# Seven block products for the output matmuls of the last pass of a retention and two-layer MLP kernel

## The chip, the core and the metric

One core of a Trainium2 chip runs the kernel. The engines are TensorE (PE in the profile, with its weight loads as PEld), VectorE (DVE), ScalarE (ACT), GpSimd (POOL) and SyncE (SP), whose queue issues nearly all the DMAs. The metric is the device time of one run in microseconds, the median of several runs; lower is better.

## What is computed

A retention layer, then two MLP layers over 2304 tokens of width 512; all in float32.

```python
x = attn_out.transpose(0, 2, 1, 3).reshape(2304, 512)     # retention, 4 x 8 heads of 576 x 64
g = x @ w_gate; x = (g * sigmoid(g) * (x @ w_val)) @ w_out   # layer one, hidden width 1536
h = maximum(x @ w_in, 0); out = (h * h) @ w_out              # layer two, hidden width 2048
```

The change lies in layer two, in the product `(h * h) @ w_out` of one third of the tokens.

## The kernel before

Every float32 operand of a matmul is held as two halves in the matmul's own 32-bit format, `hi` (a cast by ACT) and `lo` (source minus `hi`, a subtraction by DVE); `split` makes both. A product of two such operands is three matmuls: hi by hi, hi by lo, lo by hi (`three`). Inputs and results of both layers live transposed in one SBUF tile `xy`.

Layer two works in three passes of 768 tokens, each over eight systems, k = 0 to 7, of 256 hidden columns. A system's 512-deep product with `w_in` is done by Strassen's scheme in Winograd's form: seven block products P1 to P7 (`slot`), each of six matmuls of 384 columns, in the PSUM tiles `g`, `z` and `v`. The seven weight operands `wi` of a system were built in the first pass and stored in DRAM (`win`); the later passes load them one system ahead into two buffers each. After each block product ACT or DVE moves the sum out of PSUM into `cag` and `cbg` (one for the first 384 tokens, one for the others); the last two, P4 and P3, are followed by relu and square. `hidden` then splits the two halves of the tokens into `ho_hi` and `ho_lo`.

The output product is plain: `out2` takes the hidden columns of two systems (512 of them, four rows of 128) and 128 tokens, and makes twelve matmuls of 512 columns in one bank `oacc`, with weights `wo` (split once, stored as `wsp`); one instruction then adds the bank to `xy` (for the first pair, ACT copies it). A pair of systems has six such tiles, `which` "a" or "b" by j = 0 to 2. They are emitted among the block products of the following systems, by the table `outs`; the last pair's come after the last system.

The order on each engine is fixed when the program is built: the code's order, rearranged by a scheduler that goes by its own estimate of times. On the chip every engine takes its instructions in that order and waits at each one until its operands are ready.

In the names below, S0 to S7 are the eight systems of the last pass. The numbers behind names in the order listings only tell tiles apart.

Of the kernel before, what the change touches and what calls it, by code (L numbers as in the profile page):

```python
# [9 lines left out]
F32 = mybir.dt.float32  # L10
F32R = mybir.dt.float32r
U16 = mybir.dt.uint16
U32 = mybir.dt.uint32
# [48 lines left out]
def retention_moe_kernel(  # L62
# [16 lines left out]
        )  # L79

    keep = pool(ctx, "keep", 1)
    raw_p = pool(ctx, "raw_p", 2)
    cv_p = pool(ctx, "cv_p", 3)
    mid = ExitStack()
    ctx.enter_context(mid)
    cv2_p = pool(mid, "cv2_p", HOLD - 2)
    wb_p = pool(mid, "wb_p", 2)
    raw2_p = pool(mid, "raw2_p", 1)
# [286 lines left out]

    later = []
    wi_p = pool(ctx, "wi_p", 2, side="right")
    s1_p = pool(ctx, "s1_p", 1, side="right")
    xs_p = pool(ctx, "xs_p", 4, side="right")
    xo_p = pool(ctx, "xo_p", 1, side="right")  # L380

    with ExitStack() as st:
        const = pool(st, "const", 1)
# [226 lines left out]
    chain["on"] = False  # L610


    c4_p = pool(ctx, "c4_p", 1, side="right")
    ps_g2 = pool(ctx, "ps_g2", 1, space=PSUM)
    ps_a = pool(ctx, "ps_a", 1, space=PSUM)
    late = True
# [32 lines left out]
    def slot(n, i):  # L649
# [2 lines left out]
        m = M[ph]  # L652
        s = sys_.setdefault(n, {})

        if i == 1:
# [106 lines left out]
    def out2(n, which, j):  # L762

        ph, p, k, what = systems[n]
        t0 = TOKENS[ph, p]["ab".index(which)] + j * P
        final = n == len(systems) - 1 and which == "b" and j == 2
        for at in (slice(0, 256), slice(256, 512)) if final else (slice(0, 512),):
            o = out_bank()[:, at]
            for r in range(4):
                w = wos[2 * k - 2 + r]  # L770
                h = [x[:, r % 2, j * P:(j + 1) * P] for x in hid[n - 1 + r // 2, which]]
                three(o, h, (w[:, 0, at], w[:, 1, at]), r == 0, r == 3)
            home = xy[:, at.start // P:at.stop // P, t0:t0 + P]
            src = o.rearrange("p (c q) -> p c q", q=P)
            if k == 1:
                act.copy(home, src)
            else:
                tt(out=home, in0=src, in1=home, op=ALU.add)
            if k == F2 // 2 - 1:
                sp.dma_start(out=out[t0:t0 + P, at].rearrange("p (c q) -> p c q", q=P), in_=home)  # L780

    flip = systems.index((2, 0, 0, "i"))
    outs, fetch = {}, {}
    for n, (ph, p, k, what) in enumerate(systems):
        if what == "v":
            for x, which in enumerate("acb" if p == 0 else "ab"):
                at = n + 3 if which == "b" and n < flip - 1 else n + 2
                outs.setdefault(at, []).extend((out1, n, which, cc) for cc in range(CC))
            for f in range(2):
                fetch.setdefault((n, 1 + f), []).append((n, (2 * k + f,)))  # L790
        if what == "i":
            fetch.setdefault((n + 1 + (k + p == 0), 0), []).append((n, range(2 * k, 2 * k + 2)))
        if what == "i" and k % 2:
            for x, which in enumerate("ab"):
                outs.setdefault(n + 2 + x, []).extend((out2, n, which, j) for j in range(3))

    def after(n, i):

# [13 lines left out]
    place[:] = [dve.last, dve.last]  # L812
    pumped["limit"] = 10 ** 6
    end = len(systems)
    for n in range(end + 4):
        ph, p, k, what = systems[n] if n < end else (0, None, 0, "")
        tiles = outs.get(n, [])
        cuts = [len(tiles) * x // 3 for x in range(4)] if n != flip + 1 else [0] + 3 * [len(tiles)]
# [20 lines left out]
            spare.clear()  # L839
        for x in fetch.get((n, 0), []):  # L840
            load_out(*x)
        for x in seq:
            if x in (0, 1, 2):
                for y in fetch.get((n, x), []) if x else ():
# [5 lines left out]
            if n == flip + 1 and i == 4:  # L850
                while min(raw_t, default=len(order)) < loads["shut"] or min(w_t, default=len(order)) < loads["shut"]:
                    next(convert)
                mid.close()
                ho_p = pool(ctx, "ho2_p", 3)
                wo_p = pool(ctx, "wo2_p", 8)
            if not 0 <= k < end:
                continue
            if isinstance(i, tuple):
# [2 lines left out]
                slot(k, i)  # L861
            next(make, None)
            place[:] = place[1:] + [dve.recent]
            if (ph, p) in PACE:
                first, early, later_ = PACE[ph, p]
                pace["due"] += early if n - systems.index((ph, p, 0, ("gv", "i")[ph - 1][0])) < first else later_
                pump(int(pace["due"]))
                pace["due"] %= 1
            after(k, i)
        for _ in make:  # L870
            pass
        if (ph, p) == (2, 0) and systems[n + 1][1]:
            for _ in convert:
                pass


# [59 lines left out]
```

## Time and profile before

| | us |
|---|---|
| median of three runs | 874.51 |
| the three runs | 874.38, 874.51, 875.0 |
| span of the profiled execution | 875.1 |
| PE busy in it | 863.9 |
| DVE, ACT, POOL busy in it | 642.8, 400.9, 122.2 |
| longest wait of PE in it | 2.2 |

The span of the profiled execution is 0.6 us over the median of the runs; the slowest of them is about as long as it. In the rows, times are microseconds unless marked ns, and a matmul's duration contains its way through the array: the next one starts long before it has ended, so pitches are read from start to start.

### The profile page before, as it was taken

To read this page: it belongs to the slowest core of one execution; us is meant where nothing else is said; L and a number is where in the kernel's file an instruction comes from. 1 tells how busy PE (TensorE), PEld (TensorE's weight loads), DVE (VectorE), ACT (ScalarE), POOL (GpSimd) and SP (SyncE) were. 2 spreads that over 40 slices of the span, in tenths; PEclk is the share of its full clock that TensorE was granted. 3 is DMA by queue.
4 is the path that set the end of the run, shared out by engine and by line. 5 is a ranking of instruction groups with operands and counts; after the bars stand their busy time and mean duration, and the time that the engine had idled before them with its cause. 6 is when DMAs were issued, how large, how long until landed. Compare 5 with 4: busy or idle time off the path is not lost.

```text
span 875.1 us, 13516 instructions
## 1 busy us (share of the span) xinstructions
PE 863.9 (99%) x5064; PEld 746.0 (85%) x5064; DVE 642.8 (73%) x1002; ACT 400.9 (46%) x709; POOL 122.2 (14%) x135
## 2 busy tenths in 40 slices
PE   9989999999999999999999999999999999999998
PEld 7878888888888888888888899989899988998987
DVE  3899999998976899677647999999534467533544
ACT  3657777565544544644325466554233233232310
POOL 3343343223130010000002311120000000000000
PEclk9999999999999999999999999999999999999999
DMA  9994777755554489878745388988666465656412
GB/s 337 402 356 160 253 249 249 264 186 211 196 192 154 139 282 379 297 273 288 253 141 185 144 315 328 361 304 313 206 239 215 126 226 210 190 202 204 164 41 73
DMA packets 75218, 203.62 MB, mean 233 GB/s; under 512 B 7696, under 2 KB 18448, under 8 KB 75152
## 3 DMA queue, kind: packets, MB, share of 16 engines
q1 hardware_dynamic: 74720, 202.34, 65.8%
q8 instruction: 40, 0.66, 0.3%
q10 hardware_dynamic: 432, 0.41, 0.1%
q14 instruction: 26, 0.21, 0.1%
HBM read 138.23 MB, written 64.49 MB: 232 GB/s over the span
## 4 chain that ended last, share of the span: by engine, by line
PE 86%; DVE 7%; DMA 4%; issue 2%; ACT 1%; SPq 0%; POOL 0%; DVEq 0%; POOLq 0%; ACTq 0%
PE oacc L113 42%; PE g L113 24%; PE v L113 12%; PE z L113 6%; DVE w L113 3%; DMA qk_sb<-in_qk 3%; DVE wi L113 1%; PE o L113 1%; DMA k_sb<-in_kv 1%; DMA qs_sb<-in_qscale 1%; PE s L113 1%; DVE xy L113 1%; DVE cbg L113 0%; PE kv L113 0%; DVE xo_l L113 0%
## 5 line engine op out<-in xcount | busy, mean ns | idle before, releaser
L113 PE MATMUL g<-xo_h,wi 128*128 128x384 f32 (+1 forms) x768 | 238.3, 364 | 0.0
L113 PE MATMUL oacc<-wo,ho_hi 128*128 128x512 f32 (+1 forms) x584 | 179.5, 388 | 0.0
L113 PEld LDWEIGHTS g<-xo_h,wi 128*128 128x128 f32 x768 | 142.5, 188 | 17.1
L113 PE MATMUL oacc<-ho_hi,wo 128*128 128x512 f32 (+1 forms) x480 | 151.1, 370 | 0.5 <-ACT xy L113 0.5
L113 DVE TENSOR_TENSOR xy<-oacc,xy 128x512 f32<-128x512 f32 (+1 forms) x155 | 99.6, 648 | 59.6 <-PE oacc L113 59.1
L113 PE MATMUL g<-xo_l,wi 128*128 128x384 f32 (+1 forms) x384 | 139.6, 364 | 0.0
L113 PEld LDWEIGHTS oacc<-wo,ho_hi 128*128 128x128 f32 x584 | 108.4, 188 | 19.2
L113 PE MATMUL v<-xo_h,wi 128*128 128x512 f32 (+1 forms) x384 | 123.2, 364 | 0.0
L113 PE MATMUL oacc<-wo,ho_lo 128*128 128x512 f32 (+1 forms) x292 | 113.3, 390 | 0.0
L113 PEld LDWEIGHTS oacc<-ho_hi,wo 128*128 128x128 f32 x480 | 88.1, 188 | 17.6 <-ACT xy L113 1.3
L113 PE MATMUL oacc<-ho_lo,wo 128*128 128x512 f32 (+1 forms) x240 | 89.1, 371 | 0.0
L113 PEld LDWEIGHTS g<-xo_l,wi 128*128 128x128 f32 x384 | 72.1, 188 | 8.4
L113 DVE TENSOR_SCALAR w<-w 128x512 f32<-128x512 f32 (+1 forms) x136 | 64.9, 480 | 18.0 <-ACT w L113 17.0
L113 PEld LDWEIGHTS v<-xo_h,wi 128*128 128x128 f32 x384 | 71.2, 188 | 8.0
L113 DVE TENSOR_TENSOR cbg<-v,cbg 128x384 f32<-128x384 f32 (+1 forms) x72 | 43.1, 598 | 45.8 <-ACT cbg L113 24.3
L113 ACT ACTIVATE cag<-g 128x384 f32<-128x384 f32 (+1 forms) x36 | 19.0, 528 | 125.2 <-PE g L113 125.1
L113 PE MATMUL v<-xo_l,wi 128*128 128x512 f32 (+1 forms) x192 | 69.8, 363 | 0.0
L113 PEld LDWEIGHTS oacc<-wo,ho_lo 128*128 128x128 f32 x292 | 54.8, 188 | 11.2
L113 PE MATMUL z<-xo_h,wi 128*128 128x512 f32 (+1 forms) x192 | 62.5, 365 | 0.0
L113 ACT CAST ho_hi<-cbg 128x768 fp32r<-128x768 f32 (+1 forms) x36 | 32.7, 908 | 45.5 <-DVE cbg L113 44.4
L113 DVE SCALAR_TENSOR_TENSOR w<-raw,w 128x512 uint32<-128x512 uint32 x68 | 52.5, 773 | 0.7
L113 PEld LDWEIGHTS oacc<-ho_lo,wo 128*128 128x128 f32 x240 | 45.1, 188 | 8.7
(90 smaller groups left out, 1295.6 us busy)
## 6 DMA issues: line engine op xcount, KB each, us to landing
wi<-win SPq DMA_DIRECT2D x84, 512.0 KB, 4.2
raw<-in_w SPq DMA_DIRECT2D x68, 512.0 KB, 4.9
win<-wi SPq DMA_DIRECT2D x60, 512.0 KB, 3.6
wo<-wsp SPq DMA_DIRECT2D x44, 512.0 KB, 6.4
wsp<-wo SPq DMA_DIRECT2D x28, 512.0 KB, 5.2
qk_sb<-in_qk SPq DMA_DIRECT2D x15, 576.0 KB, 7.4
wst<-w SPq DMA_DIRECT2D x32, 256.0 KB, 6.0
wi<-win SPq DMA_DIRECT2D x28, 256.0 KB, 5.4
```

Source lines behind the costliest of these rows:

```text
L113: i = op(*args, **kw)
```

## The change

In the last pass, the output product of the first three pairs of systems (`PAIRED = 6`) is done with Winograd's seven block products too; the fourth pair stays plain. Hidden columns and output columns are cut in two, and so are the tokens: block j pairs 128 tokens of the first half with the 128 of the second. For each block there are seven products of six matmuls with 256 columns (`out3`), 126 matmuls in place of a pair's 72. The stationary sides are seven sums of the hidden blocks: POOL makes four of them, in four additions in a row for each block j (`sums2`, into a part of `xy` that is free by then), and `prepare` splits the seven in three pieces of 512, 256 and 1024 columns into `hs_h` and `hs_l`, of which there are two sets. The moving sides `wt` are weights and sums of weights: three slices of `wsp`, and four sums that POOL makes during the second pass (`operand_sums`), which are split and stored to DRAM there (`tsp`). Each product leaves a running sum in one half of a PSUM bank, which DVE adds to `xy` (ACT copies some of the first pair's) before the next product may go on in it.

The hidden tiles of the last pass, `caa` and `cab`, get pools of their own, opened when the second pass's tiles are given up; so the last system of the second pass is now finished before S0's tiles are written. Once the output tiles of the second pass are through, the 21 moving operands of the first three systems are loaded in a row (256 KB each). The block products of S0 to S3 stand ahead of the output products: `flow` lets the first of them go 25 slots into the pass, then three for every two slots. The fourth pair has `out4`, as `out2` before, with `whole` for its splits.

```diff
+PRODUCTS = (1, 5, 6, 3, 7, 2, 4)
+SUMS = (6, 5, 4, 7)
+PAIRED = 6
+START = 4
...
+        if i == 1 and n >= turn_over:
+            s["x"] = bank("g")[:, :m]
+            s["a"], s["b"] = block_tiles(n)
...
     def hidden(n, which, c):
+        if n >= turn_over:
+            return
...
+    def operand2(n, i):
+        w = moving[n, i] = t_p.tile([P, 2, 256], F32R, tag=f"t{i}", name="wt")
...
+    def operand_sums(n):
+        sums(n)
+        yield
+        yield
+        for x in range(4):
+            w = cv_p.tile([P, 512], U32, tag="w", name="tw").bitcast(F32R).rearrange("p (y q) -> p y q", y=2)
+            split(w[:, 0], w[:, 1], raw_o[n][x // 2][:, x % 2 * 256:][:, :256])
+            yield
+            soon(2, lambda x=x, w=w: sp.dma_start(out=tsp[systems[n][2]][:, x], in_=w.bitcast(F32)))
+            if x == 3 and systems[n][2] + 1 < PAIRED:
+                fetch_raw(n + 1)
+
+    def sums2(n, j):
+        a, b = (x[:, :, :, j * P:(j + 1) * P] for x in pairs_of[n])
+        a11, a12, a21, a22 = (x[:, :, f] for x in (a, b) for f in range(2))
+        sums_of[n, j] = s = xy[:, :, 2 * P * j:2 * P * (j + 1)].rearrange("p i (s q) -> p i s q", q=P)
+        for x, y, z, op in ((0, a21, a22, ALU.add), (2, a11, a21, ALU.subtract),
+                            (1, s[:, 0], a11, ALU.subtract), (3, a12, s[:, 1], ALU.subtract)):
+            pool_e.tensor_tensor(out=s[:, x], in0=y, in1=z, op=op)
+
+    def prepare(n, j):
+        a, b = (x[:, :, :, j * P:(j + 1) * P] for x in pairs_of[n])
+        hi, lo = (hl_p.tile([P, 7, 2, P], F32R, tag=x, name=f"hs_{x}") for x in "hl")
+        halves[n, j] = hi, lo
+        split(hi[:, 0:2], lo[:, 0:2], a.rearrange("p s f q -> p f s q"))
+        split(hi[:, 2], lo[:, 2], b[:, :, 1])
+        split(hi[:, 3:7], lo[:, 3:7], sums_of[n, j])
+
+    def out3(n, j, at):
+        i = PRODUCTS[at]
+        if at < 2:
+            bank_ = (2, 1 + j % 2 * 2)[at == 0]
+            banks[at] = ps_a.tile([P, 512], F32, tag=f"a{bank_}", name="oacc")
+        o = banks[at % 2 if at < 6 else 0]
+        o = o[:, 256:] if i == 2 else o[:, :256]
+        x = (1, 2, 4, 5, 6, 7, 3).index(i)
+        for s in range(2):
+            hi, lo = (z[:, x, s] for z in halves[n, j])
+            th, tl = (moving[n - 1 + s, i][:, y] for y in range(2))
+            for y, (c, d) in enumerate(((hi, th), (hi, tl), (lo, th))):
+                pe.matmul(
+                    o, c, d, start=i in (1, 5, 2) and s + y == 0, stop=s == 1 and y == 2, skip_group_check=True
+                )
...
+        if k == 1 and i in (1, 5, 6, 4):
+            act.copy(home, src)
+        else:
+            tt(out=home, in0=src, in1=home, op=ALU.add)
...
+    def ready_halves():
+        while queue and prepared["n"] < flowed["out"] + 2:
+            n, j = queue.pop(0)
+            (whole if n == end - 1 else prepare)(n, j)
+            prepared["n"] += 1
...
+    begin_at = 7 * 3 + START
+    for n in range(turn_over, end + 1):
+        seq = [(1, n), (7, n - 1), (2, n), (4, n - 1), (6, n), (3, n - 1), (5, n)]
+        if n == turn_over:
+            seq = [(7, n - 1), (4, n - 1), (3, n - 1), None, (1, n), (2, n), (5, n), (6, n)]
...
+            if i == 3 and k >= turn_over and systems[k][2] % 2:
+                for j in range(3):
+                    if k < turn_over + PAIRED:
+                        sums2(k, j)
+                    queue.append((k, j))
+                ready_halves()
...
+            flow(min(int(1.5 * (slots["n"] - begin_at)), 21 * PAIRED // 2))
+            after(k, i)
+            if n == turn_over + 1 and not tiles and t_p is None:
+                second.close()
+                front.close()
+                t_p, hl_p = pool(ctx, "t_p", 3), pool(ctx, "hl_p", 2)
+                block_pools.append(pool(ctx, "cb_p", 1, side="right"))
+                for m in range(turn_over, turn_over + 3):
+                    for i_ in PRODUCTS:
+                        operand2(m, i_)
```

On PE, behind S1's last block product P3 (`v_7484`, whose last matmul is the first row), the order before has an output tile of the pair before, then S2's P5.

```order
L113 MATMUL v_7484<-xo_h_7344,wi_7342 128x384
L113 MATMUL oacc_7591<-wo_7099,ho_hi_7213 128x512 x2
L113 MATMUL oacc_7591<-wo_7099,ho_lo_7214 128x512
L113 MATMUL oacc_7591<-wo_7101,ho_hi_7213 128x512 x2
L113 MATMUL oacc_7591<-wo_7101,ho_lo_7214 128x512
L113 MATMUL oacc_7591<-wo_7236,ho_hi_7338 128x512 x2
L113 MATMUL oacc_7591<-wo_7236,ho_lo_7339 128x512
L113 MATMUL oacc_7591<-wo_7238,ho_hi_7338 128x512 x2
L113 MATMUL oacc_7591<-wo_7238,ho_lo_7339 128x512
L113 MATMUL v_7606<-xo_h_7227,wi_7417 128x384
```

In the changed kernel S1's P3 (`v_7725`) is followed by S3's P1 (`g_7825`, six matmuls), by the first output products P1 of blocks 0 and 1 (`oacc_7871` and `oacc_7978`, twelve matmuls, of which the last ones are the first rows here), by S2's P6 (`g_7732`, six), and then by the output product P5 of block 0 (`oacc_7889`).

```order
L122 MATMUL oacc_7978<-wt_7656,hs_l_7809 128x256
L122 MATMUL oacc_7978<-wt_7670,hs_h_7808 128x256 x2
L122 MATMUL oacc_7978<-wt_7670,hs_l_7809 128x256
L122 MATMUL g_7732<-xo_h_7382,wi_7723 128x384
L122 MATMUL g_7732<-xo_l_7383,wi_7723 128x384
L122 MATMUL g_7732<-xo_h_7382,wi_7723 128x384 x2
L122 MATMUL g_7732<-xo_l_7383,wi_7723 128x384
L122 MATMUL g_7732<-xo_h_7382,wi_7723 128x384
L122 MATMUL oacc_7889<-wt_7658,hs_h_7800 128x256 x2
L122 MATMUL oacc_7871<-wt_7660,hs_h_7800 128x256 x2
L122 MATMUL v_7904<-xo_h_7377,wi_7761 128x384
```

No output tile of an earlier pair is left at this place, and between P3's last matmul and the first one that needs POOL's sums (`oacc_7889`) stand 24 others.

On POOL the order before ends with the weight sums of the first pass of layer two.

```order
L113 TENSOR_TENSOR w_in_5611<-w_in_5611 128x256
L113 TENSOR_TENSOR s1_5978<-w_in_5779 128x256
L113 TENSOR_TENSOR w_in_5779<-w_in_5778,w_in_5779 128x256
L113 TENSOR_TENSOR w_in_5778<-s1_5978,w_in_5778 128x256
L113 TENSOR_TENSOR w_in_5778<-w_in_5778 128x256
```

In the changed kernel the weight sums `w_o` of the second pass follow, and then the hidden sums of the three pairs; the first pair's twelve are these, after the last `w_o`. Of block 0 they are the first, second, seventh and tenth.

```order
L122 TENSOR_TENSOR w_o_7105<-w_o_7105,w_o_7104 128x256
L122 TENSOR_TENSOR xy_78<-cab_7489 128x256
L122 TENSOR_TENSOR xy_78<-caa_7488,cab_7489 128x256
L122 TENSOR_TENSOR xy_78<-cab_7489 128x256
L122 TENSOR_TENSOR xy_78<-caa_7488,cab_7489 128x256
L122 TENSOR_TENSOR xy_78<-cab_7489 128x256
L122 TENSOR_TENSOR xy_78<-caa_7488,cab_7489 128x256
L122 TENSOR_TENSOR xy_78<-xy_78,caa_7488 128x256 x3
L122 TENSOR_TENSOR xy_78<-caa_7488,xy_78 128x256 x3
```

The scheduler has put the three blocks side by side, so that the fourth sum of block 0 has nine others in front of it.

On DVE, in the output work behind the last system, the order before has one addition for every twelve matmuls and nothing else.

```order
L113 TENSOR_TENSOR ho_lo_8261<-cbg_8095,ho_hi_8260 128x768
L113 TENSOR_TENSOR xy_78<-oacc_8278,xy_78 128x4x128
L113 TENSOR_TENSOR xy_78<-oacc_8293,xy_78 128x4x128
L113 TENSOR_TENSOR xy_78<-oacc_8308,xy_78 128x4x128
L113 TENSOR_TENSOR xy_78<-oacc_8323,xy_78 128x4x128
```

In the changed kernel there is an addition for every six matmuls, and among them stand the three subtractions of the third pair's last block (`hs_l_8634`).

```order
L122 TENSOR_TENSOR xy_78<-oacc_8541,xy_78 128x2x128
L122 TENSOR_TENSOR hs_l_8634<-caa_7919,hs_h_8633 128x512
L122 TENSOR_TENSOR xy_78<-oacc_8657,xy_78 128x2x128
L122 TENSOR_TENSOR hs_l_8634<-cab_7920,hs_h_8633 128x256
L122 TENSOR_TENSOR xy_78<-oacc_8649,xy_78 128x2x128
L122 TENSOR_TENSOR hs_l_8634<-xy_78,hs_h_8633 128x1024
L122 TENSOR_TENSOR xy_78<-oacc_8706,xy_78 128x2x128
L122 TENSOR_TENSOR xy_78<-oacc_8657,xy_78 128x2x128
```

The additions that free a PSUM half now share DVE with the splits of the next block.

## Rows read from the trace of the kernel before

**Rows 1.** The page: span, busy time of each engine, granted clock by slices.

```profile
span 875.1 us, 13516 instructions
PE 863.9 (99%) x5064; PEld 746.0 (85%) x5064; DVE 642.8 (73%) x1002; ACT 400.9 (46%) x709; POOL 122.2 (14%) x135
PEclk9999999999999999999999999999999999999999
```

**Rows 2.** PE's waits, the longest: total, times, longest.

```profile
PE s L113 <- DMA qk_sb<-in_qk: 2.6, 2, 2.2
...
PE oacc L113 <- ACT xy L113: 0.9, 3, 0.4
```

**Rows 3.** Stretches: busy time by engine (instructions), granted clock, DMA share, GB/s.

```profile
720.00:740.00 20.00, 20.00 (x102) 18.10 (x101) 16.29 (x23) 8.37 (x14) 0.00 (x0) 1.00 0.61 226
...
760.00:780.00 20.00, 20.00 (x101) 17.99 (x100) 6.64 (x10) 6.25 (x12) 0.00 (x0) 1.00 0.69 232
780.00:800.00 20.00, 20.00 (x103) 18.30 (x103) 8.89 (x13) 7.69 (x13) 0.00 (x0) 1.00 0.61 198
```

**Rows 4.** Chain of work in the last pass: start, us, engine, matmuls.

```profile
740.71 5.49 PE oacc L113 x24
...
748.28 2.08 PE v L113 x12
...
756.31 2.77 PE oacc L113 x12
```

**Rows 5.** Timeline of PE in the last output tile: start, us, instruction.

```profile
868.15 0.62 PE L113 MATMUL oacc<-wo,ho_hi 128*128 128x512 f32 x2
868.60 0.39 PE L113 MATMUL oacc<-wo,ho_lo 128*128 128x512 f32 x1
868.83 0.40 PE L113 MATMUL oacc<-wo,ho_hi 128*128 128x256 f32 x2
869.06 0.28 PE L113 MATMUL oacc<-wo,ho_lo 128*128 128x256 f32 x1
869.18 0.40 PE L113 MATMUL oacc<-wo,ho_hi 128*128 128x256 f32 x2
869.42 0.28 PE L113 MATMUL oacc<-wo,ho_lo 128*128 128x256 f32 x1
```

**Rows 6.** Timeline of another system's P3: last matmul, addition, square, cast.

```profile
761.87 0.34 PE L113 MATMUL v<-xo_h,wi 128*128 128x384 f32 x1
...
762.24 0.56 DVE L113 TENSOR_TENSOR cbg<-v,cbg 128x384 f32<-128x384 f32 x1 [0.83 <-PE v L113]
...
763.58 0.95 DVE L113 SCALAR_TENSOR_TENSOR cbg<-cbg 128x768 f32<-128x768 f32 x1
...
764.62 0.84 ACT L113 CAST ho_hi<-cbg 128x768 fp32r<-128x768 f32 x1 [2.21 <-DVE cbg L113]
```

**Rows 7.** Timeline of POOL, additions of the same size: start, us.

```profile
511.67 0.74 POOL L113 TENSOR_TENSOR w_in<-w_in 128x256 f32<-128x256 f32 x1
512.49 0.74 POOL L113 TENSOR_TENSOR w_in<-s,w_in 128x256 f32<-128x256 f32 x1
513.31 1.33 POOL L113 TENSOR_TENSOR w_in<-w_in 128x256 f32<-128x256 f32 x1
527.17 1.19 POOL L113 TENSOR_TENSOR s<-w_in 128x256 f32<-128x256 f32 x1 [12.53 <-DVE cbg L113]
528.44 1.07 POOL L113 TENSOR_TENSOR w_in<-w_in 128x256 f32<-128x256 f32 x1
```

**Rows 8.** Groups by form: count, busy us, mean ns, idle before.

```profile
L113 DVE TENSOR_TENSOR ho_lo<-cbg,ho_hi 128x1024 fp32r<-128x1024 f32 x12 | 14.7, 1226 | 0.1
L113 ACT CAST ho_hi<-cbg 128x1024 fp32r<-128x1024 f32 x12 | 12.6, 1052 | 11.4 <-DVE cbg L113 11.2
L113 DVE TENSOR_TENSOR wo<-wo 128x512 fp32r<-128x512 f32 x16 | 10.7, 681 | 0.2 <-ACT wo L113 0.2
L113 ACT CAST wo<-wo 128x512 fp32r<-128x512 f32 x16 | 9.8, 621 | 1.5 <-DMA wo<-wst 1.4
L113 DVE TENSOR_TENSOR xy<-oacc,xy 128x256 f32<-128x256 f32 x22 | 9.1, 419 | 4.5 <-PE oacc L113 4.5
L113 DVE TENSOR_TENSOR wb<-w,wb 128x256 fp32r<-128x256 f32 x12 | 5.2, 436 | 0.6 <-ACT wb L113 0.6
```

**Rows 9.** Stretches with much DMA, columns as in rows 3.

```profile
530.00:535.00 5.00, 5.00 (x27) 4.49 (x26) 5.00 (x10) 3.08 (x6) 1.46 (x2) 1.00 1.02 408
700.00:705.00 5.00, 5.00 (x27) 4.53 (x26) 3.68 (x5) 1.10 (x2) 0.00 (x0) 1.00 0.82 270
```

More of the change, by code (lines that the diff above doesn't have):

```diff
@@ L610, in retention_moe_kernel @@
     chain["on"] = False
-    c4_p = pool(ctx, "c4_p", 1, side="right")
+    c4_p = pool(blocks, "c4_p", 1, side="right")
     ps_g2 = pool(ctx, "ps_g2", 1, space=PSUM)
@@ new lines, in out2, with block_tiles @@
+        if k == F2 // 2 - 1:
+            sp.dma_start(out=out[t0:t0 + P].rearrange("p (c q) -> p c q", q=P), in_=home)
+    pairs_of, block_pools = {}, []
+    def block_tiles(n):
+        k = systems[n][2]
+        if k % 2 == 0:
+            home = block_pools[k // 2 % 2]
+            pairs_of[n] = pairs_of[n + 1] = [
+                home.tile([P, 2, 2, M[2]], F32, tag=f"g{x}", name=f"ca{x}") for x in "ab"
+            ]
+        return [x[:, k % 2] for x in pairs_of[n]]
+    moving, raw_o = {}, {}
@@ new lines, in prepare @@
+    def prepare(n, j):
[5 more added lines that the diff above has]
+        split(hi[:, 3:7], lo[:, 3:7], sums_of[n, j])
+    banks = {}
+    def out3(n, j, at):
+        ph, p, k, what = systems[n]
+        i = PRODUCTS[at]
[12 more added lines that the diff above has]
+                )
+        which, half = {1: (0, 0), 5: (1, 1), 6: (0, 1), 3: (0, 1), 7: (1, 1), 2: (0, 0), 4: (1, 0)}[i]
+        t0 = TOKENS[ph, p][which] + j * P
+        home = xy[:, 2 * half:2 * half + 2, t0:t0 + P]
+        src = o.rearrange("p (c q) -> p c q", q=P)
+        if k == 1 and i in (1, 5, 6, 4):
+            act.copy(home, src)
+        else:
+            tt(out=home, in0=src, in1=home, op=ALU.add)
@@ L814, in retention_moe_kernel @@
     end = len(systems)
-    for n in range(end + 4):
+    for n in range(turn_over):
         ph, p, k, what = systems[n] if n < end else (0, None, 0, "")
@@ L871, in retention_moe_kernel @@
             pass
+        for _ in make2:
+            pass
         if (ph, p) == (2, 0) and systems[n + 1][1]:
@@ L874, in retention_moe_kernel @@
                 pass
+    due(10 ** 6)
+    stream = [
+        (n, j, at) for n in range(turn_over + 1, turn_over + PAIRED, 2) for j in range(3) for at in range(7)
+    ]
+    stream += [(end - 1, j, at) for j in range(3) for at in "ab"]
+    flowed, queue, prepared = {"n": 0, "out": 0}, [], {"n": 0}
+    def ready_halves():
[3 more added lines that the diff above has]
+            prepared["n"] += 1
@@ new lines, in follow, with flow @@
+    def follow(n, j, at):
+        if at in ("a", "b"):
+            out4(n, at, j)
+        else:
+            out3(n, j, at)
+            if j == 2:
+                for m in (n + 2, n + 3):
+                    if m < turn_over + PAIRED:
+                        operand2(m, PRODUCTS[at])
+        if at in (6, "b"):
+            flowed["out"] += 1
+            ready_halves()
+    def flow(upto):
+        while flowed["n"] < min(upto, len(stream)):
+            follow(*stream[flowed["n"]])
+            flowed["n"] += 1
@@ new lines, in retention_moe_kernel @@
+    slots["n"] = 0
+    begin_at = 7 * 3 + START
+    for n in range(turn_over, end + 1):
+        tiles = outs.get(n, [])
+        seq = [(1, n), (7, n - 1), (2, n), (4, n - 1), (6, n), (3, n - 1), (5, n)]
+        if n == turn_over:
+            seq = [(7, n - 1), (4, n - 1), (3, n - 1), None, (1, n), (2, n), (5, n), (6, n)]
+        make = build(n + 1) if n + 1 < end else iter(())
+        for x in fetch.get((n, 0), []):
+            load_out(*x)
+        for x in seq:
+            if x is None:
+                blocks.close()
+                block_pools.append(pool(ctx, "ca_p", 1, side="right"))
+                continue
+            i, k = x
+            if k == end:
+                continue
+            slot(k, i)
+            if i == 3 and k >= turn_over and systems[k][2] % 2:
[3 more added lines that the diff above has]
+                    queue.append((k, j))
+                ready_halves()
+            next(make, None)
+            if tiles:
+                fn, *args = tiles.pop(0)
+                fn(*args)
+            slots["n"] += 1
+            flow(min(int(1.5 * (slots["n"] - begin_at)), 21 * PAIRED // 2))
[8 more added lines that the diff above has]
+                        operand2(m, i_)
+        for fn, *args in tiles:
+            fn(*args)
+        for _ in make:
+            pass
+        if n == end - 1:
+            load_last(n)
@@ L878 @@
+    flow(len(stream))
 _OUT = ((NT, DM), "float32")
```

108 lines of the change are left out of this document (86 added, 22 removed).

## The prediction

> **What bounds the kernel now.** I read the page first: PE is busy 863.9 of 875.1 us, no other engine is near that, and the granted clock is at its full level in every slice [rows 1]. PE's waits come to a few microseconds in all; the longest is 2.2 us, at the start, and all waits of output matmuls on ACT together are 0.9 us [rows 2]. In the stretches of the last pass PE is busy all the time, while DVE has 6.6 to 8.9 us of work in twenty, ACT 6.3 to 7.7 and POOL none, and the DMA share is 0.6 to 0.7 [rows 3]. So here PE sets the pace, without a gap: whatever shortens its stream shortens the kernel by as much, and whatever makes it stand still is paid in full, since nothing later has slack to give back. The two questions are how much shorter the stream gets, and where the new order makes PE wait.
>
> **What PE saves.** The chain of waits has 24 plain output matmuls of 512 columns in 5.49 us, a pitch of 0.229, and twelve block product matmuls of 384 columns in 2.08, a pitch of 0.173 [rows 4]. For 256 columns the last tile has starts at 868.83, 869.06 and again 869.18, 869.42: three in 0.36 us, a pitch of 0.12 [rows 5]. A pair now takes 72 x 0.229 = 16.5 us and will take 126 x 0.12 = 15.1 us; over three pairs that is -4.05 us. An eighth of the columns goes (6.3%, not 12.5%, is left of it in time because each matmul also costs some 13 ns beside its columns). The pitch of 512 is 0.227 in the last tile (three in 0.68 us, rows 5) and 0.231 in the tile of 2.77 us [rows 4], so the bounds are -3.5 and -4.6 us.
>
> A rule that speaks against this: the Trainium skill, TensorE: Matmul & The Clock Gate, Back-to-back issue gap, gives for streams of weight loads and matmuls 131 ns per matmul at 512 columns and 81 ns at 128. By it, a plain pair would be 72 x 0.131 = 9.4 us and the block products at least 126 x 0.081 = 10.2 us, so the change would lose. The rows say 229 ns at 512, and 120 ns at 256; the measurement decides, and the sum goes by the rows.
>
> **Where PE will wait: the first sums.** The dense part of the new order has one place that the old one has not. S1's P3 is the last thing that the first pair's hidden blocks wait for. From the start of P3's last matmul (call it T) the old trace gives the way: DVE's addition starts 0.37 us later and takes 0.56, the square of 768 columns takes 0.95 [rows 6], so the blocks are there at T + 1.95. Then POOL makes the sums, ten additions until block 0's fourth, all in line on one engine. One addition of this size takes 0.74 us and the next starts 0.82 us after it; beside DVE work they take 1.07 to 1.33, and the pitch at 527 us is 1.27 [rows 7]. At 0.82 the fourth sum is ready at T + 10.2. ACT's cast of 1024 columns is 1.05 us [rows 8], so that `oacc_7889`, the first matmul with a sum, can start at T + 11.4, handovers included. PE gets there after 24 matmuls: 12 x 0.173 + 12 x 0.12 and P3's last one, T + 3.7. PE takes its instructions in order, so it stands still for 7.7 us. With ten additions at 1.2 it would be 11.5. DVE still has some 3.3 us of work in that time, the splits of block 0 and 1 (two of 0.68, two of 0.44, and S2's and S3's additions), so a few of the ten fall on the slow end: I take **+8.4 us**, ends +7.7 and +11.5.
>
> That POOL and DVE slow each other is in the rows by the spread of one shape (0.74 to 1.33 us). The Trainium skill, SBUF — State Buffer, Who interferes with whom, says that a DVE instruction with two SBUF inputs and a POOL instruction that reads SBUF block each other entirely, whoever starts first. Both of DVE's splits here are of that kind; by it each would push POOL back by its own length, about 2.2 us for the four, and the wait would be 9.9 us.
>
> **The same place, by DMA.** On SP's queue stand the 21 moving operands, and behind them `wi` for S2's P6 and P7, all behind the store of the second pass's last tile. That store can go about eleven block products (11 x 1.04 = 11.4 us) ahead of the end of P3. Then 0.26 MB of it, 19 x 0.26 and 2 x 0.52 MB make 6.3 MB; at 408 GB/s [rows 9] that is 15.4 us, and with its way S2's P6 can start at about T + 6, where PE arrives at T + 2.7. Since P6 takes only 1 us and the sums hold PE until T + 11.4 anyway, this wait lies inside the other one and costs nothing. Without the cover it would cost 3.3 us. At the 270 GB/s of a mixed stretch [rows 9] the transfers take 23 us, P6 starts at T + 13.5, and DMA is the later one.
>
> **The tail.** In the old order the tail had one addition of 0.69 us in 2.74 us of matmuls. In the new one some 22 block products, 0.72 us each, follow each other with nothing between. A block asks DVE for seven additions of 0.42 (2.94 us) and three subtractions of 0.68, 0.44 and 1.23 (2.35 us), 5.3 us [rows 8], and PE for 42 x 0.12 = 5.04: DVE, which was idle half of the time, is the bound there by a little. Three PSUM halves in turn leave 0.72 to 1.44 us between two uses of one, enough for 0.28 + 0.42 and two handovers, but not for an addition that stands behind the subtraction of 1.23: about 0.6 us at two places, 1.2 us. There are also just two sets of `hs_h` and `hs_l`. A third block's splits can begin only when the last product of the block before the previous one is out, and in three places (pair two's third block, pair three's second and third) PE comes to them after one other product, 0.84 us after that product's last start; cast and subtraction of the first piece need 0.31 + 0.62 + 0.68 and a handover, 1.65 us; two matmuls with `hi` alone fill 0.24. That is 0.6 us, three times: 1.8 us. Together **+3.0 us**; below, +1.0 if the scheduler's interleaving hides two of three, above, +4.5 if every block of the tail pays.
>
> **Edits at nothing.** In the second pass POOL gets 24 additions (it had none in that time), ACT 24 casts of 256 columns, DVE 24 subtractions of 0.44 us and SP 12 loads and 24 stores of 256 KB. DVE's fullest twenty microseconds there hold 16.3 us of work [rows 3] and get 1.8 us more; DMA gets about 100 GB/s on 226, against 408 when full [rows 9]. SP's stores wait for DVE with the `wi` loads of the next system behind them, which have a system of 15 us to come. I take 0, up to +1.0 if a load comes late. The last system of the second pass finished before S0's tiles: output tiles stand between, 0. The end, last addition and store, is the same as before, 0. S0 to S3 without output products: each block product lasts 1.04 us, and its evacuation 0.5, in other banks, 0.
>
> **The sum.** 875.1 - 4.05 + 8.4 + 3.0 = 882.45 against the profiled execution. That one is 0.6 us above the median of the runs, so **882 us**, 0.9% slower. All low ends give 878.6, all high ones 888.
>
> **Rivals.** *Covered, and faster.* If PE finds the first sums ready, the saving stays: 870.5 us, or 873.5 with the tail's waits. It speaks for it that POOL has nothing else to do. Against it stands the chain: with 1.95 us before POOL and 1.2 behind it, PE's 3.7 us leave ten additions half a microsecond. The wait is 10q - 0.5 for a pitch q, so the kernel is faster only for q under 0.15 us, where the shortest row is 0.74. Its chance, 0.09, is that I read the dependence wrongly.
>
> *The clock falls in the wait.* Nothing in the trace shows what a wait of 8 us does: after the longest, of 2.2 us, the clock is still granted in full [rows 1, 2]. If it fell to the 1.2 GHz level, matmuls would take twice as long; for as much work afterwards as the time lost, that is up to half of 8 us, +4: 886 us. The Trainium skill, TensorE: Matmul & The Clock Gate, What's actually happening, says that the gate opens by activity and closes when the engine idles; no run here shows it at a pause of this length. Chance 0.18, since P6 lies in the middle of the wait.
>
> *DMA decides.* At 270 GB/s PE waits until T + 13.5 for P6 and then for nothing: 13.5 - 2.7 = 10.8 us in place of 8.4, 884.5 us. Slices of 250 KB with rows of 1 KB, nine of the 21, speak for it; the 408 of a stretch with many loads of that size against it. Chance 0.08.
>
> *It does not do what it says.* With 256-column matmuls at 0.13 in this mix, 126 of them are as long as the 72: no saving, 886 us; against it, the last tile [rows 5]. Chance 0.03.
>
> **How the numbers follow.** My forecast, 882 with its own ends 878.6 to 886, has 0.62. With the rivals of the same sign, 0.29, slower by over 0.2% (1.75 us, about what a measurement of this kernel can tell) comes to 0.86 after some halving of both waits is set aside; faster has 0.09; within 0.2%, where only half of the wait and none of the tail is real, 0.05. The range 878 to 888 leaves out the faster case, the middle and a bit of the top.
>
> **What would show it.** Right: PE's waits have `oacc` waiting for ACT's `hs_h` or POOL's `xy` for some 8 us in one piece, near 770 us; twelve POOL additions in a row at 0.8 to 1.2 us lie just before; P6 of S2 stands alone inside the gap. The rest of the pass has 256-column matmuls at 0.12, and in the last 35 us small gaps of PE on DVE that add to about 3 us. Wrong: PE without a gap near 770 (then the kernel is faster), POOL additions much shorter than 0.7 us, or a granted clock under 1 behind the gap. If the first wait is for a DMA of `wi`, the place is right and the cause is the third rival.

## The result: 1.35% slower, and the profile after

The changed kernel takes 887.09 us (median of four runs, 886.81 to 888.59) against 874.75 of the kernel before, run beside it; the ratio is 1.0135, with a 95% interval of 1.0118 to 1.0153. The forecast was 882 us, with a range of 878 to 888.

The page of the changed kernel, its span, PE's busy time and the granted clock by slices, answers to [rows 1]:

```profile
span 885.3 us, 14201 instructions
PE 866.2 (98%) x5226; PEld 754.0 (85%) x5226; DVE 676.1 (76%) x1082; ACT 415.6 (47%) x756; POOL 169.2 (19%) x195
PEclk9999999999999999999999999999999999989999
```

One slice near the end has lost clock, which none had before. The execution of this page was timed at 887.32 us, so 2.0 us lie outside its span. The trace of before has a longer wait for `qk_sb` at its start [rows 2], and that differs from one execution to the next. Traces are therefore compared below from the first matmul of layer one's first `z` tile to the end of the last matmul. Before, that is from 80.58 to 871.86, 791.3 us; after, from 78.29 to 881.93, 803.6 us. The difference, 12.3 us, is that of the runs. Each version has one trace, so figures by the trace are those of one execution.

PE's waits of the changed kernel (total, times, longest), as [rows 2]:

```profile
PE g L122 <- DMA wi<-win: 7.0, 1, 7.0
...
PE oacc L122 <- DVE xy L122: 1.6, 4, 0.6
...
PE oacc L122 <- DVE hs_l L122: 1.2, 4, 0.4
```

There is one long wait, and its name is that of a load. The timeline of PE shows the place (start, us, instruction, in brackets the idle time before it and what ended it). The first row is the last matmul of S1's P3, the moment that the prediction calls T; then come S3's P1, twelve output matmuls, and at 775.06 S2's P6:

```profile
763.57 0.34 PE L122 MATMUL v<-xo_h,wi 128*128 128x384 f32 x1
764.04 0.44 PE L122 MATMUL g<-xo_h,wi 128*128 128x384 f32 x1
...
765.19 0.63 PE L122 MATMUL oacc<-wt,hs_h 128*128 128x256 f32 x4
766.15 0.39 PE L122 MATMUL oacc<-wt,hs_l 128*128 128x256 f32 x1 [0.33 <-DVE hs_l L122]
...
767.29 0.38 PE L122 MATMUL oacc<-wt,hs_l 128*128 128x256 f32 x1 [0.41 <-DVE hs_l L122]
...
767.75 0.28 PE L122 MATMUL oacc<-wt,hs_l 128*128 128x256 f32 x1
775.06 0.69 PE L122 MATMUL g<-xo_h,wi 128*128 128x384 f32 x1 [7.03 <-DMA wi<-win]
775.54 0.52 PE L122 MATMUL g<-xo_l,wi 128*128 128x384 f32 x1
775.87 0.84 PE L122 MATMUL g<-xo_h,wi 128*128 128x384 f32 x2
```

From T to P6 are 11.49 us, in which PE does 7 x 0.1737 + 12 x 0.12 = 2.66 us of work: 8.8 us are lost here. POOL's sums in the same stretch, the first and the last of twelve:

```profile
765.57 1.11 POOL L122 TENSOR_TENSOR xy<-cab 128x256 f32<-128x256 f32 x1 [106.25 <-DVE cab L122]
...
773.24 2.08 POOL L122 TENSOR_TENSOR xy<-caa,xy 128x256 f32<-128x256 f32 x3
```

The tenth addition, block 0's fourth sum, is the first of the three at 773.24 and is out at 773.95 (T + 10.4). ACT's casts of the sums, of blocks 0 and 1, in its timeline:

```profile
773.99 1.99 ACT L122 CAST hs_h<-xy 128x1024 fp32r<-128x1024 f32 x2 [5.55 <-POOL xy L122]
```

The first of them ends at about 775.04, T + 11.5. The load has landed by 775.06, when P6 starts. Two chains that have nothing to do with each other end in the same place within 0.02 us, and the profile names the one that came last. The load's own way, on SP's queue: the first of the 21 operand loads, the store of the second pass's last tile, and S2's two `wi` loads behind the last operand:

```profile
750.66 0.58 SPq L122 DMA_DIRECT2D wt<-wsp  x1
...
753.22 0.54 SPq L122 DMA_DIRECT2D out<-xy  x1
...
767.73 1.06 SPq L122 DMA_DIRECT2D wi<-win  x2
```

The stretches around the pause (busy time of PE, PEld, DVE, ACT, POOL, then granted clock, DMA share, GB/s, as in [rows 3]):

```profile
750.00:768.00 18.00, 17.14 (x95) 15.81 (x93) 9.74 (x16) 5.02 (x11) 2.43 (x3) 1.00 0.97 307
768.00:775.00 7.00, 0.03 (x1) 0.00 (x0) 1.97 (x3) 1.39 (x3) 7.00 (x10) 0.69 1.05 384
775.00:780.00 5.00, 4.94 (x17) 4.94 (x18) 2.48 (x2) 1.46 (x3) 0.32 (x1) 0.50 1.00 395
780.00:790.00 10.00, 10.00 (x67) 10.00 (x66) 3.26 (x7) 2.68 (x6) 0.00 (x0) 0.96 0.28 89
```

The DMA engines are full for 30 us. The granted clock falls while PE stands still and is 0.50, the 1.2 GHz level, for the first five microseconds in which PE works again: matmuls of 384 columns then start 0.32 us apart, not 0.17. From 775.06 to 781.54 PE takes 6.48 us for twelve matmuls of 384 columns and fourteen of 256, which are 3.8 us at full clock; 2.7 us are lost. The mean clock of the four runs is 0.994 to 0.996.

The third place is the tail. Four pieces of the chain of waits there:

```profile
823.78 4.21 PE oacc L122 x35
...
828.06 0.63 ACT hs_h L122
...
828.71 0.70 DVE hs_l L122
...
829.46 0.62 PE oacc L122 x3
```

35 matmuls of 256 columns in 4.21 us are a pitch of 0.120, as [rows 5] had said. Then PE stands for a block's cast and subtraction. There are six stops from 829 to 867 us, in which the next matmul starts 0.33 to 0.72 us late, 3.0 us in all. By PE's waits two of them are for `hs_l` (0.4 us together) and four for DVE's additions to `xy` (1.6 us); the other 1.0 us lies outside these waits. The matmul behind a stop takes 0.1 us longer, and with the plain tiles of the end, which run between such stops, the tail loses 4.2 us.

### The profile page after: what moved, and what is told of

The parts are those of the page before. It is cut to its first block, busy times and chain, and to the rows that moved or that the text cites. A ratio compares the mean times of both kernels' runs of the same rounds, so it can differ in the third digit from the quotient of the medians.

```text
span 885.3 us, 14201 instructions
## 1 busy us (share of the span) xinstructions
PE 866.2 (98%) x5226; PEld 754.0 (85%) x5226; DVE 676.1 (76%) x1082; ACT 415.6 (47%) x756; POOL 169.2 (19%) x195
## 4 chain that ended last, share of the span: by engine, by line
PE 82%; DVE 8%; DMA 7%; issue 1%; ACT 1%; POOL 0%; SPq 0%; DVEq 0%; POOLq 0%; ACTq 0%
PE oacc L122 40%; PE g L122 24%; PE v L122 12%; PE z L122 6%; DMA qk_sb<-in_qk 3%; DVE w L122 3%; DVE wi L122 1%; DVE xy L122 1%; DMA wi<-win 1%; DMA wt<-wsp 1%; DMA qs_sb<-in_qscale 1%; DMA k_sb<-in_kv 1%; DMA wt<-tsp 1%; PE o L122 1%; DMA v_sb<-in_kv 1%
## 5 line engine op out<-in xcount | busy, mean ns | idle before, releaser
L122 PE MATMUL g<-xo_h,wi 128*128 128x384 f32 (+1 forms) x768 | 242.3, 366 | 7.2 <-DMA wi<-win 7.0
L122 DVE TENSOR_TENSOR xy<-oacc,xy 128x512 f32<-128x512 f32 (+1 forms) x194 | 112.4, 586 | 57.9 <-PE oacc L122 57.2
L122 PE MATMUL oacc<-wo,ho_hi 128*128 128x512 f32 x384 | 119.6, 392 | 0.0
L122 PEld LDWEIGHTS oacc<-wo,ho_hi 128*128 128x128 f32 x384 | 71.5, 188 | 12.3
L122 PE MATMUL oacc<-wo,ho_lo 128*128 128x512 f32 x192 | 74.8, 394 | 0.0
L122 ACT ACTIVATE raw<-raw 128x512 uint32<-128x512 uint16 x68 | 46.0, 676 | 13.8 <-DMA raw<-in_w 13.8
L122 PE MATMUL oacc<-wt,hs_h 128*128 128x256 f32 x252 | 48.5, 289 | 1.1 <-DVE xy L122 1.1
L122 DVE CUSTOM_DVE_ANT_0 w<-raw,w 128x1024 uint16<-128x1024 uint16 x68 | 48.3, 710 | 0.8
L122 DVE TENSOR_TENSOR cbg<-v,cbg 128x384 f32<-128x384 f32 (+1 forms) x56 | 34.1, 610 | 17.2 <-PE v L122 10.1
```

Of the source, the lines that this page charges most:

```text
L122: i = op(*args, **kw)
```

## The experiments

All are timed against the kernel before, which took 874.65 to 875.49 us beside them.

### Is it the pause that costs the clock?

In `out3`, behind the product's own matmuls:

```diff
+        if n == turn_over + 1 and j == 1 and i == 1:
+            for _ in range(52):
+                with tc.issue_after(pe.recent):
+                    pe.matmul(
+                        banks[0][:, 256:], halves[n, j][0][:, 0, 0], moving[n, 1][:, 0], start=True, stop=True,
+                        skip_group_check=True
+                    )
```

Its extra matmuls also overwrite part of what block 1's outputs add up.

> The changed kernel plus 52 matmuls of 256 columns behind block 1's first product, into the half of its bank that a later product starts afresh: 6.2 us of work, at the 0.12 us pitch, in the 7.0 us in which PE waits for S2's P6. The waits stay as they are. Theory (the pause itself lowers the clock; matmuls behind it ran at half pace until 780.9 us and lost 3.2 us): clock 1.00 throughout, about 884 us, 3 us under the changed kernel's 887.1. Rival (the matmuls behind the pause are slow for another reason, such as the full DMA load): no gain, 887.

It took 885.37 us (ratio 1.0128, 1.0103 to 1.0154), 1.7 less than the changed kernel by the medians. Its trace is of the shortest of its four runs (884.37); by it, 800.2 us go from `z` to the end, 3.4 less. PE's timeline and the stretches of this run:

```profile
768.07 6.40 PE L122 MATMUL oacc<-wt,hs_h 128*128 128x256 f32 x52
775.72 0.44 PE L122 MATMUL g<-xo_h,wi 128*128 128x384 f32 x1 [1.25 <-DMA wi<-win]
776.00 0.34 PE L122 MATMUL g<-xo_l,wi 128*128 128x384 f32 x1
```

```profile
768.00:775.00 7.00, 6.47 (x54) 6.27 (x53) 2.21 (x3) 0.68 (x1) 7.00 (x11) 1.00 1.03 374
775.00:780.00 5.00, 4.28 (x29) 4.28 (x30) 2.47 (x2) 2.65 (x6) 0.65 (x1) 1.00 1.03 409
```

P6 waits for the same load, and starts even 0.5 us later after T (763.77 here), but the clock stays at 1.00 and the matmuls behind it go at full pace, at the same DMA share of 1.03. So it was the pause that cost the clock, and not the load on DMA. From P6 to the end this run is 3.7 us shorter: 2.7 of it are the clock, the rest is a tail with five stops in place of six. The Trainium skill, TensorE: Matmul & The Clock Gate, What's actually happening, says that activity opens the gate and idling closes it; these two runs agree.

### The loads alone

The added lines after the dots stand at the end of the loop over `n`.

```diff
-                for m in range(turn_over, turn_over + 3):
-                    for i_ in PRODUCTS:
-                        operand2(m, i_)
+                for i_ in PRODUCTS:
+                    operand2(turn_over, i_)
...
+        if turn_over < n < turn_over + 3:
+            for i_ in PRODUCTS:
+                operand2(n, i_)
```

> The changed kernel with the 21 operand loads dealt out: S0's seven where all 21 stood, S1's and S2's seven each a system later, so that the two loads of S2's input weights are issued 14 loads earlier. T is the start of the last matmul of S1's P3. Theory (two waits end at the same time, the loads and the ten POOL additions with their cast, each at T + 11.5): the wait for the load goes, PE now does five block products and twelve output matmuls after T (T + 7.9) and then waits some 3.6 us for the cast of the sums; 887.1 - 3.6 = 883.5, or 880.5 if the clock holds in the shorter pause. Rival (the load alone decides, the sums would be in time): the whole pause and the clock's loss go, 876.7.

881.23 us (1.0076, 1.0054 to 1.0098). The wait for `wi` is 1.1 us, and the sums are the next in line, as the PE row and the stretch behind it say:

```profile
776.92 1.74 PE L122 MATMUL oacc<-wt,hs_h 128*128 128x256 f32 x6 [2.94 <-ACT hs_h L122]
```

```profile
777.00:783.00 6.00, 6.00 (x25) 5.98 (x26) 2.38 (x2) 2.04 (x4) 0.16 (x1) 0.50 1.04 403
```

T is 764.51 here, so the sums are there at T + 12.4. The theory of two waits holds: with the load early, PE still stands 2.9 us for POOL's sums, and behind that pause the clock fell. The trace is of the longest of the four runs (884.16 us, mean clock 0.994); the other three took 880.54 to 881.67 us at a mean clock of 0.996 to 0.998. So what such a pause costs in clock differs from one execution to the next.

### The sums alone

```diff
-            pool_e.tensor_tensor(out=s[:, x], in0=y, in1=z, op=op)
+            (dve if j == 0 and n == turn_over + 1 else pool_e).tensor_tensor(out=s[:, x], in0=y, in1=z, op=op)
```

> The changed kernel with the four sums of the first pair's first block on DVE in place of POOL; the loads as in the changed kernel. Theory (two waits at the same place): PE still waits for S2's P6, now after 26 output matmuls in place of twelve; the pause is some 6.5 us, the clock falls as before, 886 to 887 us. Rival (the sums alone decide): the pause goes and with it the clock's loss, 877.

887.03 us (1.0139, 1.0120 to 1.0157), the time of the theory, but not by its way. What ends the pause is the cast of the sums that were to be early:

```profile
775.43 0.80 PE L122 MATMUL oacc<-wt,hs_h 128*128 128x256 f32 x2 [6.52 <-ACT hs_h L122]
```

DVE's timeline tells why. Its additions of 256 columns take 0.95 us while POOL works on the other blocks, and the splits' subtractions stand among them:

```profile
768.03 0.95 DVE L122 TENSOR_TENSOR xy<-cab 128x256 f32<-128x256 f32 x1
768.90 0.94 DVE L122 TENSOR_TENSOR xy<-caa,cab 128x256 f32<-128x256 f32 x1
...
773.36 0.94 DVE L122 TENSOR_TENSOR xy<-caa,xy 128x256 f32<-128x256 f32 x1
```

The fourth sum is out at 774.3, T + 9.9, half a microsecond earlier than on POOL. So this run says nothing for or against the load; it says that DVE is no quicker a place for sums beside a busy POOL.

### Both

The two diffs above together.

> The changed kernel with both edits: the operand loads dealt out by system, and the first block's four sums on DVE. Theory (two waits at the same place, and a clock that falls only because of the pause): no pause over 1 us near 770 us, clock 1.00, 887.1 - 7.8 - 3.2 = 876.1 us, with the tail's stalls of 3 to 4 us left. Rival (a third wait stands behind them, such as the DVE work that now lies before the splits): a pause of 2 to 4 us stays, 878 to 882.

880.23 us (1.0064, 1.0041 to 1.0086). The clock holds (0.999 in the mean), and the rival has it: P6 still waits for its load, and 1.0 us go to the cast of sums behind it.

```profile
765.73 0.44 PE L122 MATMUL g<-xo_h,wi 128*128 128x384 f32 x1 [1.97 <-DMA wi<-win]
```

The two loads of `wi` stand 14 loads earlier on SP's queue than in the changed kernel and are issued at 757.02, not 767.73; yet P6 starts 8.7 us after that. The DMA engines are nearly full here too (share 0.94, 313 GB/s from 750 to 768 us). Whether loads ahead of it or behind it hold the load up, this run doesn't tell.

### Order of loads and of sums

The loads at the end of the loop over `n`, and in `sums2` each addition behind the one before it:

```diff
-            pool_e.tensor_tensor(out=s[:, x], in0=y, in1=z, op=op)
+            with ExitStack() as st:
+                if j or x != 0:
+                    st.enter_context(tc.issue_after(pool_e.recent))
+                pool_e.tensor_tensor(out=s[:, x], in0=y, in1=z, op=op)
...
-                for m in range(turn_over, turn_over + 3):
-                    for i_ in PRODUCTS:
-                        operand2(m, i_)
...
+        if turn_over < n < turn_over + 4:
+            for i_ in PRODUCTS:
+                operand2(n - 1, i_)
```

> The changed kernel with S0's seven operand loads a system later too (so that the loads of S2's input weights stand ahead of most of them), and the ten POOL additions made block by block, the first block's four first, still all on POOL. T is the start of the last matmul of S1's P3. Theory (order of loads and order of sums make the pause): the first block's sums are ready at T + 6 and cast at T + 7.2, where PE comes to them at T + 8 or later; the load is there about 2.5 us earlier than in the last version; pause under 1 us, full clock: 887.1 - 7.8 - 3.2 = 876 us. Rival (DMA cannot bring all that is asked for in these 20 us): a wait of 2 us or more for wi stays, 878 or more.

877.49 us (1.0019, 1.0003 to 1.0034), 792.7 us from `z` to the end: 10.9 of the 12.3 us are back. All sums are on POOL again, but block 0's four come first, and its cast begins at 771.80. PE's waits from 700 us on are no more than these:

```profile
PE oacc L122 <- DVE xy L122: 1.6, 4, 0.5
...
PE z L122 <- DMA wi<-win: 1.0, 1, 1.0
...
PE oacc L122 <- DVE hs_l L122: 0.2, 1, 0.2
```

So the pause was one of order, on two queues: the same loads and the same additions, put otherwise, are in time but for 1.0 us.

### The tail

```diff
-PRODUCTS = (1, 5, 6, 3, 7, 2, 4)
+PRODUCTS = (1, 2, 5, 6, 3, 7, 4)
...
-        hi, lo = (hl_p.tile([P, 7, 2, P], F32R, tag=x, name=f"hs_{x}") for x in "hl")
+        ha, la, hb, lb, hc, lc = (
+            hl_p.tile([P, w, 2, P], F32R, tag=f"{x}{w}", name=f"hs_{x}") for w in (2, 1, 4) for x in "hl"
+        )
...
```

So a set of `hs_h` and `hs_l` comes free in three parts, the first after two of a block's seven products.

> The changed kernel; of the tail alone: each set of hs_h and hs_l is three tiles (two operands of a, one of b, the four sums) in place of one, and product 2 stands second in a block in place of sixth, so that the first tile of a set is free after two of seven products. Theory (the tail's stalls of 3.8 us come from just two sets: a block's casts start when the block before the last one is out): most of the stalls go, the wait near 770 us and its clock stay, 884.5 us. Rival (DVE's pace sets the tail): the stalls move to waits for DVE's additions and the time stays at 887.

886.9 us (1.0136, 1.0112 to 1.0160): no gain. My theory, that two sets of `hs_h` and `hs_l` are too few, finds no support: the waits for `hs_l` are gone, and those for DVE's additions grow from 1.6 us to 2.3. Put on top of the last version, the edit makes it worse, from 877.49 to 879.6 us:

> Both: loads later, sums by block, and the tail's tiles in three parts with product 2 early. If both theories hold the changes add: 876 - 2.5 = 873.5 us, a little under the kernel before (874.6). If DVE sets the tail, 876. If loads still make PE wait, 878.

(1.0047, 1.0030 to 1.0063.) Its waits for DVE's additions are 3.1 us. What DVE does at such a stop is seen in the version with loads and sums in order. DVE's timeline:

```profile
845.42 0.69 DVE L122 TENSOR_TENSOR hs_l<-caa,hs_h 128x512 fp32r<-128x512 f32 x1
846.03 0.42 DVE L122 TENSOR_TENSOR xy<-oacc,xy 128x256 f32<-128x256 f32 x1
846.37 0.41 DVE L122 TENSOR_TENSOR hs_l<-cab,hs_h 128x256 fp32r<-128x256 f32 x1
846.70 0.42 DVE L122 TENSOR_TENSOR xy<-oacc,xy 128x256 f32<-128x256 f32 x1
847.03 1.21 DVE L122 TENSOR_TENSOR hs_l<-xy,hs_h 128x1024 fp32r<-128x1024 f32 x1
848.17 1.08 DVE L122 TENSOR_TENSOR xy<-oacc,xy 128x256 f32<-128x256 f32 x3
```

and PE's, where the next product waits for the first of the three additions at 848.17:

```profile
848.73 0.47 PE L122 MATMUL oacc<-wt,hs_h 128*128 128x256 f32 x2 [0.39 <-DVE xy L122]
```

An addition that would free a PSUM bank stands behind a subtraction of 1.21 us. So I cut the long subtraction and gave the last pair a fourth bank:

```diff
-        split(hi[:, 3:7], lo[:, 3:7], sums_of[n, j])
+        act.copy(hi[:, 3:7], sums_of[n, j])
+        for x in range(4):
+            dve.tensor_tensor(
+                out=lo[:, 3 + x], in0=sums_of[n, j][:, x], in1=f32(hi[:, 3 + x]), op=ALU.subtract
+            )
...
+            if at and j % 2 and n == turn_over + PAIRED - 1:
+                bank_ = 0
```

> The last version with later loads and sums by block (877.5 us), and of the tail: the subtraction of the four sums (1024 columns, 1.22 us) made in four of 256 columns, so that additions that free PSUM banks can go between, and a fourth bank for the last product pair's second block. Theory (additions stand behind long subtractions on DVE, and PE behind the bank that they would free): the six stalls of 0.3 to 0.7 us, 2.9 us in all, shrink to about 1 us, 875.5 us. Rival (DVE has too much work there, in whatever pieces): four pieces cost 0.3 us more per block than one, the stalls stay, 877.5 to 879.

877.76 us (1.0027, 1.0016 to 1.0039), no better. The stops of the tail shrink from 2.9 to 2.2 us, but the first pair, where POOL works beside DVE, now stops PE for 1.1 us for `hs_l`, and S2's P6 waits 0.9 us for its load. Whether pieces or DVE's amount of work decide the tail stays open.

### Leave the tail plain

Here only the first two pairs go by products; the rest is the version with loads and sums in order.

```diff
-PAIRED = 6
+PAIRED = 4
...
+    stream += [(n, j, at) for n in range(turn_over + PAIRED + 1, end, 2) for j in range(3) for at in "ab"]
...
+        if n in (turn_over + 1, turn_over + 2, turn_over + 4):
+            for i_ in PRODUCTS:
+                operand2(min(n - 1, turn_over + 2), i_)
```

The last lines put S2's loads a system later. The plain third pair's four `wo` tiles are loaded into the operands' buffers as these come free.

> The last version with later loads and sums by block, with only the first four systems by block products of 256 columns and the last four plain (their operands in the buffers of the products; S2's seven operands loaded a system later). Theory (a pair saves 1.35 us of PE's stream and a pair that ends in the tail gives that back in stalls, as DVE is the bound there): two pairs save 2.7 us, the tail's stalls fall from 3.0 to under 0.7, the wait of 1.2 us for wi goes as well; 874.6 - 2.7 + 0.7 = 872.6 us, ahead of both kernels. Rival (the third pair pays after all): 877.5 + 1.35 = 878.9.

874.91 us (0.9999, 0.9991 to 1.0008): level with the kernel before. From `z` to the end it takes 790.7 us, 0.6 less than before. Behind 790 us the profile lists no wait of PE, and the only one of the pass is for a load:

```profile
PE z L122 <- DMA wi<-win: 1.2, 1, 1.2
```

By the pitches two pairs save 2.7 us; of the 2.1 that are gone again 1.2 are this wait, the rest are smaller delays. The third pair by products is thus worth less than nothing: the version that has it is 2.6 us slower by the medians (877.49) and 2.0 by the traces. It also has S2's loads a system earlier, but its wait for a load, 1.0 us, is not the longer one.

The last wait is for a load again. Dealing the first operands out product by product, four at the end of S1's turn and then one after each block product:

```diff
+            if n > turn_over + 1 and loads_:
+                operand2(*loads_.pop(0))
...
-        if n in (turn_over + 1, turn_over + 2, turn_over + 4):
-            for i_ in PRODUCTS:
-                operand2(min(n - 1, turn_over + 2), i_)
+        if n == turn_over + 1:
+            loads_ = [(m, i_) for i_ in PRODUCTS for m in (turn_over, turn_over + 1)]
+            loads_ += [(turn_over + 2, i_) for i_ in PRODUCTS]
+            for _ in range(4):
+                operand2(*loads_.pop(0))
```

> The last version (four systems by products, later loads, sums by block; 874.9 us against 874.9 of the kernel before) with the first pair's 14 operand loads dealt out product by product, four at once and then one per block product, so that the load of S4's first input weights stands three loads (0.75 MB, 2 us at 380 GB/s) earlier. Theory (PE's last wait, 1.3 us for that load, is one of DMA's order): the wait goes, 873.6 us, 0.15% ahead of the kernel before. Rival (DMA brings no more in that stretch, whatever the order): another load comes late in its place, 874.9.

874.53 us against 875.49 beside it (0.9992, 0.9981 to 1.0002), 790.2 us by the trace. The wait for `wi` is gone; 0.7 us now go to the sums' cast and 0.3 to a load of `wo`. By the trace that is 1.1 us ahead of the kernel before, by the runs it cannot be told from it. No version here beats it measurably.

## Point by point: why the prediction was right, and where it was short

- **PE's saving, -4.05 us: right.** The pitch of 256 columns is 0.120 in the last pass too (35 matmuls in 4.21 us). Taking from 803.6 us all by which matmuls start later than their pitch and did not before, 16.3 us, leaves 787.3, 4.0 under before. That "6.3%" of a pair's time is saved was misread: 1.35 of 16.5 us are 8%; the sum doesn't use it.
- **The wait for the first sums, +8.4: right in size (8.8), half right in cause, and in part by luck.** T + 1.95 for the blocks (measured T + 2.0), T + 10.2 for the fourth sum (T + 10.4) and T + 11.4 for its cast (T + 11.5) all held; alone, they would have held PE for 11.5 - 3.7 = 7.8 us (an estimate from these rows). But what PE stood for was P6's load, the prediction's own sign for its third rival (chance 0.08). That the load came at the same moment as the cast is chance: in the same order on PE an earlier one would have left 7.8 us, a later one would have cost more. By the rule of the Trainium skill, SBUF — State Buffer, Who interferes with whom, as I had priced it, the sums would have cost 9.9 us; 7.8 is nearer to the price from the rows.
- **DMA at the same place, "costs nothing": wrong, with little effect on the sum.** I had the load there at T + 6, or T + 13.5 at the lower rate; it came at T + 11.5. The step that failed is the transfer's price, 6.3 MB at 408 GB/s. The store ahead of it went at T - 10.3, 1.1 us later than I had it, and from there to P6 it took 21.8 us, not 17.4. From 750 to 775 us the engines were full at 307 and then 384 GB/s, 329 in the mean; at that rate 6.3 MB take 19.1 us in place of 15.4 (an estimate from these rows). Where the other 0.7 us went, and why the rate was lower than the 408 of [rows 9], no run shows. So neither cover hid the other; both had to go (runs of the loads alone, and of order).
- **The clock, given 0.18 as a rival: it was so, +2.7 us.** The forecast had it at nothing and should have had it in its sum. I had counted on S2's P6 in the middle of the wait; P6 was itself what waited.
- **The tail, +3.0: 4.2 us.** PE's listed waits there are all for DVE; whether its order or its amount of work is the bound stays open. The six stops are 3.0 us; I left out the 0.1 us by which a matmul behind a stop is longer, and the plain tiles between stops. The two sets, 1.8 us of my sum, are not borne out: only 0.4 us of the waits are for `hs_l`, and freeing the sets earlier gained nothing.
- **Edits at nothing: right.** From 140 to 763 us the profile lists no wait of PE in the changed kernel; the weight sums of the second pass cost no time that shows.
- **The base of the sum, without effect.** The 0.6 us between span and median compare unlike things: a run's time is 1.7 to 2.1 us longer than its span here, so the profiled execution of before was some 2 us longer than the median run. The forecast of 7.4 us over before doesn't hang on it.

The sum of what was measured is -4.05 + 8.8 + 2.7 + 4.2 = 11.7 us, and 0.6 us more are delays of about 0.1 us and less each; the runs say 12.3, the forecast said 7.4. The difference is the clock, 1.2 us of the tail, 0.4 of the pause and the small delays.

## What to carry to other kernels

Where one engine is full, price an edit that shortens its stream by the first place where its new inputs come from a slow engine or a full queue: a saving of 4 us here met 16 us of losses in one pause, its clock and a tail. If two chains end at the same wait, removing one shows the other; change both before judging either. And stop a cheaper algorithm where the work that covered its overheads stops: with the same method only on the systems that still had block products beside them the loss was gone, though no measurable gain was left.

## What the runs showed of the hardware

**DVE and POOL.** A DVE subtraction of 512 columns with both inputs in SBUF takes 1.22 us at 804.38, while POOL adds, and 0.69 at 855.36, when POOL is idle; an addition of 256 columns that takes one input from PSUM is 0.42 us either way (824.53 beside POOL, 854.83 without). DVE's timeline of the changed kernel:

```profile
804.38 1.22 DVE L122 TENSOR_TENSOR hs_l<-caa,hs_h 128x512 fp32r<-128x512 f32 x1
...
824.53 0.42 DVE L122 TENSOR_TENSOR xy<-oacc,xy 128x256 f32<-128x256 f32 x1 [1.34 <-PE oacc L122]
...
854.83 0.42 DVE L122 TENSOR_TENSOR xy<-oacc,xy 128x256 f32<-128x256 f32 x1 [1.02 <-PE oacc L122]
855.36 0.69 DVE L122 TENSOR_TENSOR hs_l<-caa,hs_h 128x512 fp32r<-128x512 f32 x1
```

The Trainium skill, SBUF — State Buffer, Who interferes with whom, says that a DVE instruction with two SBUF inputs contends with a GpSimd instruction that reads SBUF, and that one with at most one SBUF input, outside the 2-port modes, doesn't contend with GpSimd. The rows agree: 1.22 against 0.69 us, and 0.42 in both.

**The clock in a short pause.** In the trace of the loads alone the clock was 0.50 from 777 to 783 us, behind a pause of 2.9 us and with PE at work all the time. In the version with loads and sums in order it was 0.50 from 51.3 to 54.7 us behind a first wait for `qk_sb` of 1.9 us; in the trace of before one of 2.2 us at the same place left it full [rows 1, 2], as did P6's wait of 2.0 us in the run of both. The length of a wait alone doesn't tell which.
